# Rescheduling the first batch of a fused cosformer attention and gated MLP over four engines

## Chip, cores and metric

One core of a Trainium2 chip runs the whole program. The metric is device time in microseconds (us), the median of several runs. The engines named below are TensorE (PE, with its weight loads as PEld), VectorE (DVE), ScalarE (ACT), GpSimd (POOL) and SyncE (SP), which issues most of the DMAs.

## The reference

Linear attention with a cosine weighting, for 8 batches of 8 heads, 576 positions and 64 dimensions, all in fp32, is followed by a two-layer MLP on 4608 tokens of 512 features, with 2048 hidden units:

```
theta = pi/2 * pos/576
phi(x) = concat(relu(x)*cos(theta), relu(x)*sin(theta))        # 64 -> 128
kv  = phi(k)^T @ v        z = sum over positions of phi(k)
x   = (phi(q) @ kv) / (phi(q) . z + 1e-6)                        # per head, heads joined to 512
h   = x @ w_in;  g = h * sigmoid(beta*h);  out = g @ w_out
```

## The kernel before

**Layout.** Positions of a batch are written p*9 + n, with p in 0..63 and n in 0..8. A "block" is one n: 64 positions of each of two head groups g on 128 partitions. Heads come as two head pairs jp (0 and 1) with two heads jj each, times the two groups g. Tokens go through the MLP in 9 chunks of 512, that is 8 blocks; block 8 of batch 0 therefore already belongs to chunk 1.

**Attention of a batch.** `q_relu` and `k_relu` write bf16 relus of q and k (`qb`, `rk`). `v_scale` multiplies v by the cosine or the sine and writes `vb`; the 65th column of `vb` holds the weight itself and so gives z. `kv_mm` multiplies `rk` by `vb` on PE, with 64x64 tiles, into PSUM banks 6 and 7, and `kv_take` copies that to `kv`. `q_turn_pe` transposes `qb` on PE; its `take` functions copy the result to `qt` (ACT) and, multiplied by the tangent `tanr`, to `qs` (DVE). `num_mm` makes numerator and denominator of one block and head pair. `x_rden` adds epsilon to the denominator and inverts it, and `x_mul` (DVE) or `x_mul_act` (ACT) multiplies. `x_turn_pe` transposes the result on PE, and a copy by ACT or DVE brings it to `xt`, the MLP's input.

**MLP.** `h_mm` makes one of 16 h groups of a chunk (four 512-column matmuls, L374), in PSUM bank `h_bank`; `h_act` applies SiLU on ACT (L381). `o_part` makes the output: part i uses w_out i (16 matmuls at L399 over four token tiles). The weights are loaded as fp32 in four pieces each of w_in and w_out (1 MB each) into four stage buffers, cast to bf16 by `cast_win` (L106, L108) and `cast_wout` (L115, L117, which also divide by beta). `cast_win` has four calls for a piece, one for each combination gj of row halves.

**Order.** `manual_schedule` keeps each engine's instructions in program order, so the order written out by hand from L429 to L539 is the schedule; the framework adds the waits. Batch 0 is done first, up to chunk 0's first h groups. The first half of h groups 0 to 3 (head pair 0, `mis` 0 and 1) runs ahead of the second. Then a loop of 32 slots makes chunk 0: slots 0 to 15 are h groups, slots 16 to 31 output tiles. The dictionary `early` puts batch 1's work behind given slots. From chunk 1 on, `att_units` does the same for the later batches, and x reaches `xt` by DMA transposes. That part is untouched.

**Fill-ins.** `warm_pe(count, w)` issues matmuls on zeros that nobody reads, to keep PE busy (L424). SP issues all loads in order. Before w_in 1 and before w_in 2 stands a load of two elements into `gate` (L462, L464) that reads `rk`; SP waits for that relu and so delays the weight loads behind it. A w_out piece reuses a stage buffer and waits for the casts of the w_in piece in it.

Of the kernel before, what the change touches and what calls it, by code (L numbers as in the profile page):

```python
# [22 lines left out]
def kernel(  # L23
# [114 lines left out]
    for g in range(2):  # L138
        nc.gpsimd.iota(it9[g * HP : (g + 1) * HP], pattern=[[1, NQ]], base=0, channel_multiplier=NQ,
                       allow_small_or_imprecise_dtypes=True)  # L140
    halfpi = const.tile([P, 1], FP32, name="halfpi")
# [13 lines left out]
    zeros = const.tile([P, 512], BF16, name="zeros")  # L155
    nc.vector.memset(zeros, 0.0)
    ones = const.tile([HP, P], FP32, name="ones")
    nc.vector.memset(ones, 1.0)
# [4 lines left out]

    gate = const.tile([1, 2], BF16, name="gate")
# [12 lines left out]

    tdiag = const.tile([HP, NQ, HP], FP32, name="tdiag")
    nc.vector.tensor_tensor(  # L179
        tdiag, identf.unsqueeze(1).to_broadcast([HP, NQ, HP]),  # L180
        tan9[0:HP].unsqueeze(2).to_broadcast([HP, NQ, HP]), op=ALU.mult)
# [240 lines left out]
    def warm_pe(count, w=512, bank=1):  # L422
        for i in range(count):
            nc.tensor.matmul(ps[:, bank, 0:w], lhsT=zeros[:, 0:P], rhs=zeros[:, 0:w], start=True, stop=True)  # L424
# [37 lines left out]
    nc.sync.dma_start(out=gate, in_=rk[0:1, 0, 0, 0:2])  # L462
# [26 lines left out]
    got2 = x_rden(6, 0, 7, NQ, (1,))  # L489
# [13 lines left out]
    for i in range(1, 4):  # L503
        for f in (0, 256) if i == 1 else (0,):
            for gj in GJ:
                cast_win(i, gj, "dve", f, f + 256 if i == 1 else 512)
    load_w("out", 0)
    load_w("out", 1)
    load_raw(1, "v")
    load_raw(1, "k")  # L510
    load_w("out", 2)
    load_raw(1, "q")
    load_w("out", 3)
    cast_wout(0)
    cast_wout(1)
    v_scale(1, 0)
    k_relu(1)
    cast_wout(2)
    q_relu(1, 0)


    def num_seven(jp, bank):
        for n in range(7):
            num_mm(n, jp, bank, n)

    takes = []
    early = {
        4: lambda: x_turn_pe(0, 8, 9, 7),
        15: lambda: v_scale(1, 1, eng="act"),
        22: lambda: (kv_mm(1, 0, 6), kv_mm(1, 1, 6), q_relu(1, 1), kv_take((0, 1), 6)),  # L530
        24: lambda: (cast_wout(3, "aadd"), takes.append(q_turn_pe(1, 0, 4, hold=True))),
        25: lambda: (takes.append(q_turn_pe(1, 1, 6, hold=True)),
                     [takes[jp](e, i) for jp in range(2)
                      for e, i in (("act", 0), ("dve", 1), ("act", 1), ("dve", 0))]),
        28: lambda: (num_seven(0, 4), num_seven(1, 6), x_mul(x_rden(4, 0, 0, 7, (0,)), 0, 7)),
        29: lambda: (x_turn_pe(1, 0, 7, 4, ("act",), (0,)), x_mul(x_rden(6, 0, 0, 7, (1,)), 0, 7)),
# [91 lines left out]
```

## Time and profile before

| what | us |
|---|---|
| median of 7 runs | 299.25 (298.02 to 301.81) |
| profiled execution, its time | 298.59 |
| profiled execution, its span | 296.8 |
| PE busy in the span | 284.6 |
| first kv matmul (L268) starts | 12.99 |
| first h matmul (L374) starts | 18.48 |
| casts of w_in on DVE (L108) | 20.24 to 30.67 |
| first output matmul (L399) starts | 34.91 |
| w_out 3 lands | 45.13 |

The profile shows one execution. Times are counted from the span's start. In the page, busy shares are given for the whole span and for 40 slices of 7.4 us each; the chain of waits follows the last instruction back to what released it, step by step, as start and duration in us. A timeline row gives start, duration, engine, line, operation, output<-inputs, shape and count, and in brackets the idle time before it with what ended it. A row of the waits gives who waited for whom: us in total, times, longest. [...] many records overlap: 512-column matmuls of 379 ns start 216 ns apart.

### The profile page before, as it was taken

The numbers are of one execution on the slowest core, as the hardware profiler recorded it, in microseconds if no ns is written. First come the engines' busy times: TensorE is split into PE (matmuls) and PEld (weight loads), VectorE is DVE, ScalarE is ACT, GpSimd is POOL, SyncE is SP. The second block draws the span as 40 slices with busy tenths as digits, with TensorE's granted clock in tenths as the row PEclk, the third lists the DMA queues.
The fourth block names the chain that finished last, engine by engine and source line by source line (L and its number), as shares of the span: only waits on it lengthen the run. The fifth ranks groups of instructions, "written<-read, shape, count | busy, mean of one in ns | idle before, by whom it ended". The sixth has DMA issues, their size and how long they took to land.

```text
span 296.8 us, 7162 instructions
## 1 busy us (share of the span) xinstructions
PE 284.6 (96%) x3042; PEld 143.2 (48%) x3068; DVE 113.8 (38%) x282; ACT 140.9 (47%) x224; POOL 73.7 (25%) x88
## 2 busy tenths in 40 slices
PE   7969999999999999999999999999999999999994
PEld 5644455445444544445445544554455444444443
DVE  3879968572930195008600770068005000000000
ACT  6658836572148313841285127602761177127511
POOL 1550001443364034501460157014701210000000
PEclk9999999999999999999999999999999999999998
DMA  7999999698899059934993499229201910131033
GB/s 244 380 376 343 390 389 390 223 245 313 137 254 389 6 97 201 358 128 94 190 360 142 91 210 371 111 60 189 53 2 31 161 35 0 38 78 28 0 73 71
DMA packets 50264, 53.82 MB, mean 181 GB/s; under 512 B 30888, under 2 KB 31160, under 8 KB 50232
## 3 DMA queue, kind: packets, MB, share of 16 engines
q1 hardware_dynamic: 47512, 46.01, 51.7%
q0 software_dynamic: 2688, 7.34, 10.3%
q8 instruction: 24, 0.39, 0.5%
q14 instruction: 8, 0.07, 0.1%
q10 hardware_dynamic: 32, 0.01, 0.0%
HBM read 36.71 MB, written 9.44 MB: 155 GB/s over the span
## 4 chain that ended last, share of the span: by engine, by line
PE 93%; ACT 3%; issue 2%; DVE 1%; DVEq 0%; ACTq 0%
PE ps L374 41%; PE ps L399 39%; PE ps L289 4%; PE ps L268 3%; PE ps L424 1%; PE ps L415 1%; ACT g_t L381 1%; PE ps L238 1%; PE ps L348 1%; PE ps L432 1%; DVE qs L226 1%; ACT xt L353 1%; ACT L151 0%; DVE tdiag L179 0%; ACT wout L115 0%
## 5 line engine op out<-in xcount | busy, mean ns | idle before, releaser
L374 PE MATMUL ps<-xt,win 128*128 128x512 bf16 x576 | 127.8, 379 | 2.5 <-ACT xt L353 1.1
L399 PE MATMUL ps<-wout,g_t 128*128 128x512 bf16 x536 | 120.4, 379 | 2.3 <-issue 1.5
L381 ACT ACTIVATE g_t<-ps,beta 128x512 bf16<-128x512 f32 x144 | 98.4, 688 | 36.2 <-PE ps L374 36.2
L374 PEld LDWEIGHTS <-win 128*128 128x128 bf16 x576 | 55.6, 98 | 68.7 <-issue 1.8
L399 PEld LDWEIGHTS <-g_t 128*128 128x128 bf16 x560 | 54.0, 98 | 64.2 <-issue 0.5
L394 POOL DMA_DIRECT2D out_dram<-o_sb x56 | 35.0, 629 | 146.3 <-ACT o_sb L405 146.3
L405 ACT COPY o_sb<-ps 128x512 f32<-128x512 f32 x35 | 20.5, 586 | 99.0 <-PE ps L399 99.0
L226 POOL TENSOR_TENSOR qs<-qt,tanr 128x1152 bf16<-128x1152 bf16 x12 | 29.2, 2454 | 9.5 <-DVE vb L223 8.4
L280 DVE CAST kv<-ps 128x520 bf16<-128x520 f32 x7 | 4.9, 699 | 68.4 <-PE ps L268 68.4
L418 DVE COPY o_sb<-ps 128x256 f32<-128x256 f32 x1 | 0.4, 425 | 63.2 <-PE ps L415 63.2
L311 DVE TENSOR_TENSOR xs<-ps,rden 128x768 bf16<-128x768 f32 (+3 forms) x24 | 22.4, 935 | 1.0 <-DVE rden L304 0.2
L223 DVE TENSOR_SCALAR vb<-raw_v,cos 128x256 bf16<-128x256 f32 x63 | 17.1, 346 | 0.0
L300 DVE TENSOR_TENSOR den<-ps,eps 128x12 f32<-128x12 f32 (+3 forms) x25 | 4.1, 164 | 32.4 <-PE ps L289 32.2
L223 DVE TENSOR_SCALAR vb<-raw_v,sin 128x256 bf16<-128x256 f32 x54 | 14.7, 348 | 0.0
L289 PEld LDWEIGHTS <-qt 64*64 64x64 bf16 x576 | 10.5, 106 | 4.4 <-issue 3.9
L289 PE MATMUL ps<-kv,qt 64*64 64x65 bf16 x576 | 11.7, 195 | 0.3 <-DVE qs L226 0.2
L289 PE MATMUL ps<-kv,qs 64*64 64x65 bf16 x576 | 11.6, 193 | 0.2 <-issue 0.2
L198 DVE TENSOR_SCALAR qb<-raw_q 128x1152 bf16<-128x1152 f32 x15 | 10.6, 748 | 1.4 <-DMA raw_q<-in_q_dram 1.4
L289 PEld LDWEIGHTS <-qs 64*64 64x64 bf16 x576 | 10.5, 105 | 0.3 <-issue 0.3
L108 DVE CAST win<-w_stage 64x512 bf16<-64x512 f32 (+2 forms) x20 | 10.0, 501 | 0.4
L268 PEld LDWEIGHTS <-rk 64*64 64x64 bf16 x576 | 8.5, 106 | 3.4 <-issue 2.5
L198 DVE TENSOR_SCALAR rk<-raw_k 128x2304 bf16<-128x2304 f32 (+1 forms) x8 | 9.9, 1242 | 0.4 <-DMA raw_k<-in_k_dram 0.4
(58 smaller groups left out, 102.5 us busy)
## 6 DMA issues: line engine op xcount, KB each, us to landing
raw_v<-in_v_dram SPq DMA_DIRECT2D x7, 1152.0 KB, 9.9
raw_k<-in_k_dram SPq DMA_DIRECT2D x7, 1152.0 KB, 14.3
raw_q<-in_q_dram SPq DMA_DIRECT2D x7, 1152.0 KB, 7.3
out_dram<-o_sb POOLq DMA_DIRECT2D x56, 128.0 KB, 3.9
w_stage<-in_moe_w_out_dram SPq DMA_DIRECT2D x4, 1024.0 KB, 8.8
w_stage<-in_moe_w_in_dram SPq DMA_DIRECT2D x3, 1024.0 KB, 6.3
out_dram<-o_sb SPq DMA_DIRECT2D x14, 128.0 KB, 2.3
raw_q<-in_q_dram SPq DMA_DIRECT2D x2, 576.0 KB, 3.9
```

The source lines that it names most:

```text
L108: nc.vector.tensor_copy(o, a)
L198: nc.vector.tensor_scalar(dst, src, scalar1=0.0, scalar2=None, op0=ALU.max)
L223: nc.vector.tensor_scalar(o, a, scalar1=t[:, n : n + 1], scalar2=None, op0=ALU.mult)
L226: eng.tensor_tensor(dst.rearrange("q n (g p) -> q n g p", g=2), src.rearrange("q n (g p) -> q n g p", g=2), tanr[:, n0:n1].unsqueeze(2).to ...
L268: nc.tensor.matmul(t[jj * HP : (jj + 1) * HP, g], lhsT=rk[hs, n, 2 * jp + jj, :], rhs=vb[hs, n, 2 * jp + jj].rearrange("q s e -> q (s e)") ...
L289: nc.tensor.matmul(ps[cols, bank + jj, slot * E : (slot + 1) * E], lhsT=(qt, qs)[cs][rows, jp, n, cols], rhs=kv[rows, g, jp, cs, :], start ...
L311: nc.vector.tensor_tensor(o.rearrange("q j n s d -> q j (n s) d"), nv[:, :, a:z, :, 0:D].rearrange("q j n s d -> q j (n s) d"), rden[:, :, ...
L374: nc.tensor.matmul(ps[:, h_bank(c, jt)], lhsT=win[jt // 4][:, mi, (jt % 4) * P : (jt % 4 + 1) * P], rhs=xt[:, :, jp, g * HP : (g + 1) * HP ...
L381: nc.scalar.activation(g_t, ps[:, h_bank(c, jt)], AF.Silu, scale=beta[:, jt : jt + 1])
L394: eng.dma_start(out=out_v[bb, n][:, m0:m1], in_=o_sb[hf * HP : (hf + 1) * HP, m0:m1])
L399: nc.tensor.matmul(o_ps, lhsT=gs[c, jt][:, tt * P : (tt + 1) * P], rhs=wout[jt // 4][:, jt % 4, :], start=(jt == 0), stop=(jt == JT - 1))
L405: nc.scalar.copy(o_sb, o_ps)
```

## The change

The whole change lies in batch 0's part, in the setup ahead of it, and in the slots of chunk 0.

- Setup: `zeros` is filled in two pieces, the first ahead of the other constants. `ones` and `tdiag` go: the tangent is spread over partitions by nine fp32 PE transposes of a broadcast column, and DVE, not ACT, copies it to `tanr`. Both first q relus are on DVE.
- Dummies: 58 of 48 columns instead of 78 of 40; 8 instead of 5 of 128 columns ahead of the first turn; 7 instead of 9 of 512 columns ahead of the first kv; two more before the second x turn.
- k relu of heads 0 and 1 is split between ACT and DVE. POOL's second product with the sine covers blocks 0 to 4; ACT does blocks 5 to 8. kv of head pair 1 is made one head at a time.
- Block 8 leaves the first part: only block 7 is made beside blocks 0 to 6. Block 8's `num_mm` comes after slot 3 and its turn after slot 7 in bank 6. Its sum and product stand on DVE ahead of the casts of w_in 2 and 3. w_in 2 is cast in halves.
- The `gate` loads go; w_in 1 to 3 are issued right behind w_in 0.
- Batch 1: `kv_take` is on ACT; w_out 3 is cast one part on ACT and three on DVE, between the takes of head pair 0 and those of head pair 1, and no longer ahead of both; the second `num` comes after slot 29, the x turn of pair 0 after slot 30.

```diff
+    zeros = const.tile([P, 512], BF16, name="zeros")
+    nc.vector.memset(zeros[:, 0:P], 0.0)
...
-    zeros = const.tile([P, 512], BF16, name="zeros")
-    nc.vector.memset(zeros, 0.0)
-    ones = const.tile([HP, P], FP32, name="ones")
-    nc.vector.memset(ones, 1.0)
+    nc.vector.memset(zeros[:, P:512], 0.0)
...
-    tdiag = const.tile([HP, NQ, HP], FP32, name="tdiag")
-    nc.vector.tensor_tensor(
-        tdiag, identf.unsqueeze(1).to_broadcast([HP, NQ, HP]),
-        tan9[0:HP].unsqueeze(2).to_broadcast([HP, NQ, HP]), op=ALU.mult)
...
-    warm_pe(78, 40)
-    q_relu(0, 0, "act")
+    warm_pe(58, 48)
     for bank, n0, n1 in ((6, 0, 5), (7, 5, NQ)):
-        nc.tensor.matmul(ps[:, bank, 0 : (n1 - n0) * HP], lhsT=ones,
-                         rhs=tdiag[:, n0:n1, :], start=True, stop=True)
+        for n in range(n0, n1):
+            nc.tensor.matmul(ps[:, bank, (n - n0) * HP : (n - n0 + 1) * HP],
+                             lhsT=tan9[0:HP, n : n + 1].to_broadcast([HP, P]), rhs=identf,
+                             is_transpose=True, start=(n == n0), stop=(n == n1 - 1))
+    nc.tensor.transpose(ps[:, 1, 0:JT], beta16, identf[0:JT, 0:JT])
     for bank, n0, n1 in ((6, 0, 5), (7, 5, NQ)):
-        nc.scalar.copy(tanr[:, n0:n1, :].rearrange("q n p -> q (n p)"), ps[:, bank, 0 : (n1 - n0) * HP])
-    nc.tensor.transpose(ps[:, 1, 0:JT], beta16, identf[0:JT, 0:JT])
+        nc.vector.tensor_copy(tanr[:, n0:n1, :].rearrange("q n p -> q (n p)"), ps[:, bank, 0 : (n1 - n0) * HP])
+    q_relu(0, 0)
+    nc.vector.tensor_copy(beta, ps[:, 1, 0:JT])
     nc.vector.tensor_copy(ps[:, 0, 0:NQ], cos9)
     nc.vector.tensor_copy(ps[:, 0, 16 : 16 + NQ], sin9)
-    nc.vector.tensor_copy(beta, ps[:, 1, 0:JT])
+    q_relu(0, 1)
+    warm_pe(8, 128, bank=0 + 2)
+    q_turn_pe(0, 0, 4)
     nc.vector.reciprocal(rbeta, beta)
-    q_relu(0, 1, "dve")
-    warm_pe(5, 128)
-    q_turn_pe(0, 0, 4)
     warm_pe(4, 128)
     take = q_turn_pe(0, 1, 2, hold=True)
-    warm_pe(9)
+    warm_pe(7)
     take("act", 0)
+    take("dve", 1)
     v_scale(0, 1, 0, eng="pool")
+    take("act", 1)
     v_scale(0, 0, 0)
-    k_relu(0, 0, 2, "act")
-    take("dve", 1)
+    k_relu(0, 0, 2, "act", 0, 5)
+    k_relu(0, 0, 2, "dve", 5, NQ)
     take("dve", 0)
-    take("act", 1)
     kv_mm(0, 0, 6)
-    v_scale(0, 1, 1, eng="pool")
+    v_scale(0, 1, 1, 0, 5, eng="pool")
     v_scale(0, 0, 1)
     kv_take((0,), 6, eng="act")
+    v_scale(0, 1, 1, 5, NQ, eng="act")
     k_relu(0, 2, 3, "act")
-    k_relu(0, 3, 4, "dve", 0, 5)
-    k_relu(0, 3, 4, "act", 5, NQ)
-
-    nc.sync.dma_start(out=gate, in_=rk[0:1, 0, 0, 0:2])
-    load_w("in", 1)
-    nc.sync.dma_start(out=gate, in_=rk[0:1, 0, 3, 0:2])
-    load_w("in", 2)
-    load_w("in", 3)
-    warm_pe(1, bank=1)
-    for n in range(7, NQ):
-        num_mm(n, 0, 4, n - 7)
+    for i in range(1, 4):
+        load_w("in", i)
+    warm_pe(1)
     for n in range(7):
         num_mm(n, 0, 2, n)
-    kv_mm(0, 1, 6)
+    num_mm(7, 0, 4, 0)
     warm_pe(2, bank=1)
-    got2 = x_rden(4, 0, 7, NQ, (0,))
+    kv_mm(0, 1, 6, (0,))
+    k_relu(0, 3, 4, "act", 5, NQ)
     got = x_rden(2, 0, 0, 7, (0,))
+    got2 = x_rden(4, 0, 7, 8, (0,))
+    k_relu(0, 3, 4, "dve", 0, 5)
+    kv_mm(0, 1, 6, (1,))
+    x_mul_act(got2, 7)
     kv_take((1,), 6, eng="act")
     x_mul(got, 0, 7)
-    x_mul_act(got2, 7)
-    x_mul_act(got2, 8)
-    for n in range(7, NQ):
-        num_mm(n, 1, 6, n - 7)
     for n in range(7):
         num_mm(n, 1, 0, n)
+    num_mm(7, 1, 6, 0)
     for gj in GJ:
-        cast_win(0, gj, "pool", jps=slice(0, 1))
+        cast_win(0, gj, "act" if gj == (1, 1) else "pool", jps=slice(0, 1))
...
     x_turn_pe(0, 0, 8, 2, jps=(0,))
-    got2 = x_rden(6, 0, 7, NQ, (1,))
     got = x_rden(0, 0, 0, 7, (1,))
     x_mul(got, 0, 4)
     x_mul(got, 4, 7)
-    x_mul_act(got2, 7)
+    x_mul(x_rden(6, 0, 7, 8, (1,)), 7, 8)
+    warm_pe(2, bank=3)
+    x_turn_pe(0, 0, 4, 4, ("act",), (1,))
     h_mm(0, 0, (0, 1))
-    x_turn_pe(0, 0, 4, 4, ("dve",), (1,))
-    h_mm(0, 1, (0, 1))
     x_turn_pe(0, 4, 8, 5, ("act",), (1,))
-    x_mul_act(got2, 8)
-    h_mm(0, 2, (0, 1))
-    h_mm(0, 3, (0, 1))
+    for jt in range(1, 4):
+        h_mm(0, jt, (0, 1))
...
+    cast_halves(1)
+    def rest():
+        x_mul(x_rden(2, 0, 8, NQ, (0, 1)), 8, NQ)
+        cast_halves(2)
+        for gj in GJ:
+            cast_win(3, gj)
+        load_w("out", 0)
...
     early = {
-        4: lambda: x_turn_pe(0, 8, 9, 7),
+        3: lambda: (num_mm(8, 0, 2, 0), num_mm(8, 1, 2, 1), rest()),
+        7: lambda: x_turn_pe(0, 8, 9, 6),
         15: lambda: v_scale(1, 1, eng="act"),
-        22: lambda: (kv_mm(1, 0, 6), kv_mm(1, 1, 6), q_relu(1, 1), kv_take((0, 1), 6)),
-        24: lambda: (cast_wout(3, "aadd"), takes.append(q_turn_pe(1, 0, 4, hold=True))),
-        25: lambda: (takes.append(q_turn_pe(1, 1, 6, hold=True)),
-                     [takes[jp](e, i) for jp in range(2)
-                      for e, i in (("act", 0), ("dve", 1), ("act", 1), ("dve", 0))]),
-        28: lambda: (num_seven(0, 4), num_seven(1, 6), x_mul(x_rden(4, 0, 0, 7, (0,)), 0, 7)),
-        29: lambda: (x_turn_pe(1, 0, 7, 4, ("act",), (0,)), x_mul(x_rden(6, 0, 0, 7, (1,)), 0, 7)),
+        22: lambda: (kv_mm(1, 0, 6), kv_mm(1, 1, 6), kv_take((0, 1), 6, "act"), q_relu(1, 1)),
+        25: lambda: takes.append(q_turn_pe(1, 0, 4, hold=True)),
+        26: lambda: (takes.append(q_turn_pe(1, 1, 6, hold=True)),
+                     [takes[0](*t) for t in turns], cast_wout(3, "addd"),
+                     [takes[1](*t) for t in turns]),
+        28: lambda: (num_seven(0, 4), x_mul(x_rden(4, 0, 0, 7, (0,)), 0, 7)),
+        29: lambda: (num_seven(1, 6), x_mul(x_rden(6, 0, 0, 7, (1,)), 0, 7)),
+        30: lambda: x_turn_pe(1, 0, 7, 4, ("act",), (0,)),
```

More of the change, by code (lines that the diff above doesn't have):

```diff
@@ L162 @@
     make_identity(nc, ident)
-    gate = const.tile([1, 2], BF16, name="gate")
     vb = one.tile([P, NQ, 4, 2, E], BF16, name="vb")
@@ L492, with cast_halves @@
     x_mul(got, 4, 7)
-    x_mul_act(got2, 7)
+    x_mul(x_rden(6, 0, 7, 8, (1,)), 7, 8)
+    warm_pe(2, bank=3)
+    x_turn_pe(0, 0, 4, 4, ("act",), (1,))
     h_mm(0, 0, (0, 1))
-    x_turn_pe(0, 0, 4, 4, ("dve",), (1,))
-    h_mm(0, 1, (0, 1))
     x_turn_pe(0, 4, 8, 5, ("act",), (1,))
-    x_mul_act(got2, 8)
-    h_mm(0, 2, (0, 1))
-    h_mm(0, 3, (0, 1))
+    for jt in range(1, 4):
+        h_mm(0, jt, (0, 1))
     for gj in GJ:
         cast_win(0, gj, "dve", 256, 512, slice(1, 2))
-    for i in range(1, 4):
-        for f in (0, 256) if i == 1 else (0,):
+    def cast_halves(i):
+        for f in (0, 256):
             for gj in GJ:
[L506 to L519, printed above, removed]
+                cast_win(i, gj, "dve", f, f + 256)
+    cast_halves(1)
[5 more added lines that the diff above has]
+        load_w("out", 0)
+        load_w("out", 1)
+        load_raw(1, "v")
+        load_raw(1, "k")
+        load_w("out", 2)
+        load_raw(1, "q")
+        load_w("out", 3)
+        cast_wout(0)
+        cast_wout(1)
+        v_scale(1, 0)
+        k_relu(1)
+        cast_wout(2)
+        q_relu(1, 0)
     def num_seven(jp, bank):
@@ L526 @@
     takes = []
+    turns = (("act", 0), ("dve", 1), ("act", 1), ("dve", 0))
     early = {
-        4: lambda: x_turn_pe(0, 8, 9, 7),
+        3: lambda: (num_mm(8, 0, 2, 0), num_mm(8, 1, 2, 1), rest()),
+        7: lambda: x_turn_pe(0, 8, 9, 6),
         15: lambda: v_scale(1, 1, eng="act"),
-        22: lambda: (kv_mm(1, 0, 6), kv_mm(1, 1, 6), q_relu(1, 1), kv_take((0, 1), 6)),
-        24: lambda: (cast_wout(3, "aadd"), takes.append(q_turn_pe(1, 0, 4, hold=True))),
-        25: lambda: (takes.append(q_turn_pe(1, 1, 6, hold=True)),
-                     [takes[jp](e, i) for jp in range(2)
-                      for e, i in (("act", 0), ("dve", 1), ("act", 1), ("dve", 0))]),
-        28: lambda: (num_seven(0, 4), num_seven(1, 6), x_mul(x_rden(4, 0, 0, 7, (0,)), 0, 7)),
-        29: lambda: (x_turn_pe(1, 0, 7, 4, ("act",), (0,)), x_mul(x_rden(6, 0, 0, 7, (1,)), 0, 7)),
+        22: lambda: (kv_mm(1, 0, 6), kv_mm(1, 1, 6), kv_take((0, 1), 6, "act"), q_relu(1, 1)),
[6 more added lines that the diff above has]
+        30: lambda: x_turn_pe(1, 0, 7, 4, ("act",), (0,)),
         31: lambda: ([h_mm(1, jt, (0, 1)) for jt in range(2)], x_turn_pe(1, 0, 7, 5, ("dve",), (1,)),
```

## The prediction

> **What bounds the kernel now.** I read four views in this order: the page's busy shares and slices, the chain of waits, the timeline of 12 to 50 us, and TensorE's and SP's lists of waits.
>
> ```profile
> PE 284.6 (96%) x3042; PEld 143.2 (48%) x3068; DVE 113.8 (38%) x282; ACT 140.9 (47%) x224; POOL 73.7 (25%) x88
> PE   7969999999999999999999999999999999999994
> DMA  7999999698899059934993499229201910131033
> PE 93%; ACT 3%; issue 2%; DVE 1%; DVEq 0%; ACTq 0%
> ```
>
> TensorE (PE) is full from the fifth slice (30 us) on, so only the first 60 us can change. Full is not useful: up to 17 us PE fills with dummies (L424). The end moves by as much as the dense stream of h groups moves. In the chain it is held like this:
>
> ```profile
> 10.33 2.73 PE ps L424 x8
> 13.06 0.66 PE ps L268 x36
> ...
> 17.41 1.02 ACT xt L353
> ...
> 21.07 0.23 ACT xs L321
> ...
> 24.55 0.71 ACT g_t L381
> ```
>
> ```profile
> PE ps L374 <- ACT xt L353: 1.1, 1, 1.1
> PE ps L374 <- ACT xs L321: 0.9, 1, 0.9
> PE ps L348 <- ACT g_t L381: 0.4, 1, 0.4
> ```
>
> First, the dummies end at 13.06, though the inputs of the first kv product (L268) are ready at 11.8 (the longest, ScalarE's relu, runs 10.63 to 11.80). Second, h waits for the first x copy (18.43). Third, h group 2 writes bank 6, which ScalarE's multiply for block 8 (L321) still reads until 21.29. Fourth, the turn of block 8 uses bank 7 and waits for h group 3's activation.
>
> ```profile
> 20.24 10.43 DVE L108 CAST win<-w_stage 64x256 bf16<-64x256 f32 x20
> 30.70 3.26 DVE L117 TENSOR_SCALAR wout<-w_stage,rbeta 128x512 bf16<-128x512 f32 x8
> ```
>
> ```profile
> SPq L462 <- ACT rk L196: 5.0, 1, 5.0
> ```
>
> VectorE (DVE) casts w_in from 20.24 to 30.67 without a break. h group 12, the first to need w_in 3, starts at 31.45: cover of only 0.8 us. This second front decides what an earlier PE is worth. SP, last, sits 5.0 us in front of its first gate load before it may issue w_in 1.
>
> [...] 512-wide dummies start 427 ns apart until 12.03 us, then 216. [...] Here landings come in order of issue, even with deep backlog (w_out 0 27.54, w_out 1 30.37, v 33.64, k 36.65, w_out 2 39.34, q 42.41, w_out 3 45.13). [...]
>
> **The change, part by part** (times of the profiled execution: span 296.8, 298.59 with what lies around it, 0.66 below the median 299.25).
>
> *Opening.* VectorE loses the 0.75 us product `tdiag` and the `ones` fill. Nine fp32 transposes replace two fp32 products (4.31 to 6.59); they can start at 3.46, after `tan9`. No row shows their price. Below: 0.107 each, the spacing of a 128-wide weight load at half clock. Above: 0.33 (fp32 load of L432) + 0.285 (L436's matmul), not overlapped, 0.6 each. I take 0.16, since loads overlap matmuls in every row here: nine end at 4.9. VectorE then copies `tanr` (0.49 + 0.43, from L418's 425 ns for 256) and does the first q relu (0.70, was 1.16 on ScalarE) by 6.2. The first turn starts at 6.27 against 7.56, the second at 7.66 against 8.95. Dummies: 7 from 8.85, at half clock 7 x 0.427, end at 11.84. ScalarE's and VectorE's shares of k relu (about 0.74 and 0.42) end by 11.3, POOL's product at 11.2. So the first kv runs at **11.85 against 12.99**: 1.15 earlier. The smaller dummy and constant moves are free: they stand before the first transpose or under the wait for it.
>
> *kv of pair 1.* ScalarE takes kv at 12.7 to 13.1, then four new v scalings: [...] 0.29 apart, to 14.25. POOL's shorter product, ended 13.1 instead of 14.04, was not what kv waited for. Behind them ScalarE has relu of head 2 (0.69, to 14.85) and part of head 3 (0.41, to 15.2). kv by single heads starts at 14.9 and ends at about 15.6, as before (15.57). **The 1.15 is spent on ScalarE here**; single heads hide only 0.3 of it. num, the turn and the x copy stand as before (copy about 17.4 to 18.4).
>
> *After num.* VectorE no longer waits for PE's turn to copy xt (idle 18.53 to 19.83, copy to 20.32). ScalarE does both copies (0.59 each), by 20.2. VectorE adds block 7's sum, inverse and product (0.15 + 0.18 + 0.29) and begins casting at **19.1 against 20.24**. Without block 8 in bank 6, the first halves of h 0 to 3 end their issue at 20.75 against 22.19. Block 8's num (16 small matmuls, 0.14) is new between h groups and waits 0.2 for bank 2, in place of the 0.52 wait in bank 7. h group 5 starts at 23.7 against 25.41: 1.7 earlier.
>
> *Casts.* VectorE now has block 8's sum and product in the middle (0.17 + 0.19 + 0.42 and gaps, 0.8), and w_in 2 in eight halves (8 x 0.44) instead of four (4 x 0.71): 0.7 more. w_in 3 ends at 19.1 + 10.43 + 1.5 = 31.0 against 30.67. PE would be at group 12 at 29.75. It waits: its second matmul, which needs the last cast, runs at 31.0 against 31.67. **Of 1.7 us, 0.7 is left; w_in 3 is what is late next.**
>
> *w_out, batch 1.* q lands at 42.4 and w_out 3 at 45.13 as before. Before, ScalarE waits 5.8 for w_out 3 ahead of the qt copies, and num of pair 1 then stands 0.37 for `qs` (start 49.30). Now pair 0's four takes go first, 44.6 to 46.2; the casts (one on ScalarE, three on VectorE) 46.0 to 47.4; pair 1's takes to 48.75. Group o 3 needs the last cast at 47.4 and reaches it then. num of pair 1 stands 49.0. The chain wins another 0.4, as the 0.37 goes and the turns fall between o groups; a wait of about 0.3 for the x copy, behind two output copies on ScalarE, is included. The kv take on ScalarE (0.59) fills idle time.
>
> *SP's loads.* The two 2-byte gate loads and their waits go; behind them stood only w_in 1 to 3 and what follows. Those now issue from 6.8. As the queue is busy to 24.35 and in order, they land as before (18.9, 21.7, 24.35): nothing won or lost. The later loads of w_out wait for the casts: w_out 3's stage slot is freed at 31.0 for 30.67, with v, k and q queued ahead, so it is hidden.
>
> *Sum.* 0.7 + 0.4 = 1.1 us at the same clock step. [...] My steps for the kernel before, summed the same way, come out 0.4 late by group 15, so those of after probably do too: 0.4 more. **1.5 us: 297.1 for a profiled execution like this one, 297.7 as a median.**
>
> **Rivals.** A change of 0.5% (1.5 us) is about what a measurement can tell from none.
>
> *Forecast, 0.45:* gain 1.1 to 2.2, both sides of that bound.
>
> *The casts take nearly all, 0.25.* If VectorE starts casting at 19.7 rather than 19.1, group 12 runs at 31.6 against 31.67; the tail's 0.4 is left: 298.9. For it: ten VectorE instructions stand on the way to 19.1, and L198 took 477 ns for 320 elements beside POOL, which could lengthen k relu. Against: VectorE's 1.3 us idle is real and goes.
>
> *PE's gain stays, 0.13.* If casts run faster or w_in 3 is reached in time, the whole 1.7 and the 0.4 remain: 297.2. Against: 10.43 us of casts without a gap.
>
> *Slower, 0.17: the opening transposes.* At 0.6 each unoverlapped they end at 8.9. The q relu queued behind `tanr` on VectorE then ends at 9.8, the dummies run into 14.9, casts start at 22.1, group 12 at 34.0: 1.9 behind, 301.1. The loss is then one for one; it starts where one transpose takes over 0.38, beyond which VectorE starts casting after 20. [...] Against: L436's weight load took 178 ns, not 330.
>
> *The loads are not in order after all* (inside the 0.17): the early w_in loads take half the rate from v, k and w_in 0. Landing 3 us later gives +1 us. Against: the ordered landings above.
>
> **How the numbers follow.** Low end 296.4: the whole 2.1, 0.4 for an early clock step, and 0.3 for the scatter of a median. High end 300.4: it takes in the late casts, the late loads, and the slower case up to some 0.5 us for a transpose (0.9 us of loss for each 0.1 beyond 0.38). Faster by over 0.5% is a bit over half of the forecast, the case where PE's gain stays, and the better end of the casts: 0.45. Within: 0.38. Slower: 0.17.
>
> **What would show it.** The first L268 near 11.9, and pair 1's kv ending near 15.6. L108 starting near 19.1. No wait of PE on L321. A new wait PE L374 <- DVE win at 29.7 to 31.0. Nine L238-like fp32 transposes 0.11 to 0.25 apart. ACT wout waiting for no DMA. Wrong if w_in 0 lands later than 16.4, if h group 12 starts after 31.5, or if PE idles after 50 us.

## The result, and the profile after

The changed kernel takes **297.5 us** in the median (296.87 to 299.15, 25 runs), against 299.05 for the kernel before beside it (297.88 to 301.81, 62 runs): ratio **0.9949, 95% interval 0.9931 to 0.9967**, a gain of 1.5 us. A second set of runs of the unchanged new kernel (e4, below) gave 0.9927 (0.9898 to 0.9957). Two runs more than 1.5% above the fastest of their kernel, one of e11 and one of the kernel before, are left out where runs are counted by their clock.

The profiled execution of the new kernel took 298.60, which is 1.1 above its own median and level with the profiled 298.59 of before. That coincidence is the first thing to explain. The page first:

```profile
PE 283.8 (96%) x3028; PEld 143.1 (48%) x3056; DVE 115.9 (39%) x292; ACT 140.1 (47%) x221; POOL 73.8 (25%) x87
...
PE   8689899999999999999999999999999999999994
...
DMA  7999999698799069915992599139201910131033
...
PE 87%; DVE 5%; DMA 3%; issue 2%; ACT 1%; SPq 1%; DVEq 0%
```

PE is full from the sixth slice on (37 us; before, from the fifth). In the chain's shares a DMA (3%) has appeared, which was not there before, and ScalarE has fallen from 3% to 1%. The chain in order of time names them:

```profile
3.42 9.77 DMA raw_v<-in_v_dram
13.25 1.24 issue
...
15.18 1.13 PE ps L260 x34
...
30.89 0.70 DVE win L108
31.64 3.41 PE ps L366 x15
...
52.19 0.92 ACT xt L345
53.16 1.02 PE ps L366 x4
```

The head of the chain is now the load of v's second half, which landed at 13.20. (It was issued at 3.42; the chain puts the whole time since then on it.) Then comes the product of pair 1's kv (L260), and later the last cast of w_in 3 (L108), for which h group 12 (L366) waits, as forecast. What v's landing holds up is read in the timeline, where the bracket gives each engine's idle time and what ended it:

```profile
13.22 1.35 DVE L205 TENSOR_TENSOR vb<-raw_v,ps 128x1152 bf16<-128x1152 f32 x1 [1.12 <-DMA raw_v<-in_v_dram]
13.26 1.26 POOL L205 TENSOR_TENSOR vb<-raw_v,sin 128x640 bf16<-128x640 f32 x1 [2.18 <-DMA raw_v<-in_v_dram]
13.28 1.28 ACT L213 ACTIVATE vb<-raw_v,sin 128x128 bf16<-128x128 f32 x4 [1.01 <-DMA raw_v<-in_v_dram]
14.46 0.97 ACT L188 ACTIVATE rk<-raw_k 128x576 bf16<-128x576 f32 x2
...
15.18 1.11 PE L260 MATMUL ps<-vb,rk 64*64 64x130 bf16 x36 [1.62 <-DVE rden L296]
```

Three engines stood idle for 1.0 to 2.2 us waiting for that one load. The bracket of the PE row names `rden`, but the work behind it is ScalarE's: four v scalings, then the relu of k's head 2, which ended at 15.13. In nine of the profiles below the product starts 0.05 us after that relu, while `rden` ended 0.01 to 0.13 before it. PE's list of waits over the first 60 us:

```profile
PE ps L260 <- DVE rden L296: 1.6, 1, 1.6
...
PE ps L366 <- DVE win L108: 0.9, 1, 0.9
...
PE ps L366 <- ACT g_t L373: 0.5, 1, 0.5
...
PE ps L366 <- ACT xt L345: 0.2, 1, 0.2
```

The waits of before for ScalarE's `xs` (0.9), of the block turn for the activation (0.4) and of the first h group for the x copy (1.1) are gone; the 0.2 listed for an x copy is batch 1's, at 53.16. The waits for v and for the last cast have replaced them.

**Two executions must be compared at the same landing of v.** In the profiles of the changed kernel with its opening kept, pair 1's kv starts 1.98 to 2.07 us after that landing (e3: 2.27), and the landing scatters between 11.58 and 13.20. The unchanged kernel's two profiles took 298.60 with the landing at 13.20 and 297.98 at 12.47: 285.40 and 285.51 behind it. The landing was at 11.86 in the profile of before, where the first kv (12.99) held the chain and not v:

```profile
11.93 2.11 POOL L213 TENSOR_TENSOR vb<-raw_v,sin 128x1152 bf16<-128x1152 f32 x1 [0.71 <-DMA raw_v<-in_v_dram]
...
12.99 0.42 PE L268 MATMUL ps<-vb,rk 64*64 64x130 bf16 x16
```

At 11.86 the changed kernel would take about 297.3, **1.3 under the 298.59 of before**. This line through two executions is an estimate, but the spread agrees: its runs at full clock lie between 296.87 and 298.60, 1.7 us, and the landings of all the profiles with this opening span 1.6. (0.1 to 0.2 of the 1.3 arises behind h(1, 4), h group 4 of chunk 1, where the two kernels are the same: from its start to the end the profiles of all kernels take 239.9 to 240.9 us.)

### The profile page after: what moved, and what is told of

It is laid out like the page before. It is cut to its first block, busy times and chain, and to the rows that moved or that the text cites. A ratio compares the mean times of both kernels' runs of the same rounds, so it can differ in the third digit from the quotient of the medians.

```text
span 296.8 us, 7134 instructions
## 1 busy us (share of the span) xinstructions
PE 283.8 (96%) x3028; PEld 143.1 (48%) x3056; DVE 115.9 (39%) x292; ACT 140.1 (47%) x221; POOL 73.8 (25%) x87
## 4 chain that ended last, share of the span: by engine, by line
PE 87%; DVE 5%; DMA 3%; issue 2%; ACT 1%; SPq 1%; DVEq 0%
PE ps L391 40%; PE ps L366 38%; DVE win L108 4%; PE ps L281 3%; DMA raw_v<-in_v_dram 3%; PE ps L260 3%; PE ps L407 1%; SPq L78 1%; DVE xs L303 0%; ACT g_t L373 0%; DVE rden L296 0%; PE ps L230 0%; ACT xt L345 0%; DVE den L292 0%; DVE o_sb L410 0%
## 5 line engine op out<-in xcount | busy, mean ns | idle before, releaser
L366 PE MATMUL ps<-xt,win 128*128 128x512 bf16 x576 | 128.0, 379 | 1.7 <-DVE win L108 0.9
L366 PEld LDWEIGHTS <-win 128*128 128x128 bf16 x576 | 55.5, 98 | 68.2 <-DVE win L108 1.8
L386 POOL DMA_DIRECT2D out_dram<-o_sb x56 | 36.4, 654 | 143.4 <-ACT o_sb L397 142.9
L272 DVE CAST kv<-ps 128x520 bf16<-128x520 f32 x6 | 4.2, 700 | 68.1 <-PE ps L260 68.1
L303 DVE TENSOR_TENSOR xs<-ps,rden 128x768 bf16<-128x768 f32 (+5 forms) x26 | 23.1, 890 | 0.8
L292 DVE TENSOR_TENSOR den<-ps,eps 128x12 f32<-128x12 f32 (+4 forms) x26 | 4.2, 160 | 33.2 <-PE ps L281 33.1
L260 PE MATMUL ps<-vb,rk 64*64 64x130 bf16 x576 | 10.3, 218 | 2.3 <-DVE rden L296 1.6
L190 DVE TENSOR_SCALAR qb<-raw_q 128x1152 bf16<-128x1152 f32 x16 | 11.4, 752 | 1.3 <-DMA raw_q<-in_q_dram 1.3
L260 PEld LDWEIGHTS <-rk 64*64 64x64 bf16 x576 | 8.9, 106 | 6.2 <-ACT rk L188 3.2
L190 DVE TENSOR_SCALAR rk<-raw_k 128x2304 bf16<-128x2304 f32 (+2 forms) x9 | 10.9, 1211 | 0.5 <-DMA raw_k<-in_k_dram 0.5
L108 DVE CAST win<-w_stage 64x512 bf16<-64x512 f32 (+2 forms) x24 | 10.7, 447 | 0.5
```

What stands on the lines that cost most here:

```text
L108: nc.vector.tensor_copy(o, a)
L190: nc.vector.tensor_scalar(dst, src, scalar1=0.0, scalar2=None, op0=ALU.max)
L260: nc.tensor.matmul(t[jj * HP : (jj + 1) * HP, g], lhsT=rk[hs, n, 2 * jp + jj, :], rhs=vb[hs, n, 2 * jp + jj].rearrange("q s e -> q (s e)") ...
L303: nc.vector.tensor_tensor(o.rearrange("q j n s d -> q j (n s) d"), nv[:, :, a:z, :, 0:D].rearrange("q j n s d -> q j (n s) d"), rden[:, :, ...
L366: nc.tensor.matmul(ps[:, h_bank(c, jt)], lhsT=win[jt // 4][:, mi, (jt % 4) * P : (jt % 4 + 1) * P], rhs=xt[:, :, jp, g * HP : (g + 1) * HP ...
L386: eng.dma_start(out=out_v[bb, n][:, m0:m1], in_=o_sb[hf * HP : (hf + 1) * HP, m0:m1])
```

## The experiments

All times are medians. The kernel before stood at 299.41 beside the first four, 299.31 beside the next four and 298.76 beside the last.

### e1, e2: do the gate loads matter?

e1 puts them back into the changed kernel (the second reads head 2's relu, where the kernel before reads head 3's); e2 takes them out of the kernel before.

```diff
+    nc.sync.dma_start(out=gate, in_=rk[0:1, 0, 0, 0:2])
     load_w("in", 1)
+    nc.sync.dma_start(out=gate, in_=rk[0:1, 0, 2, 0:2])
     load_w("in", 2)
     load_w("in", 3)
```

> The changed kernel with the two gate loads put back, so that w_in 1 waits for head 0's relu and w_in 2 and 3 for head 2's. Theory A (w_in loads issued at 6.6 us keep the DMA engines that are ahead busy and so slow those that still carry v and k): the second half of v lands at 11.9 instead of 13.2 us, VectorE starts to cast before 18.8, and the median is 0.5 to 1.0 us under the changed kernel's 297.5. Theory B ([...] v's landing only scatters from execution to execution): no change beyond 0.3 us, and v lands anywhere between 11.8 and 13.2.

> The kernel before without the two gate loads, nothing else. Theory A: v's second half lands at about 13.2, POOL's product with it ends at 15.3 instead of 14.0, kv of pair 1 moves from 15.57 to about 15.9, and the median rises by 0.2 to 1.0 us over 299.05. Theory B, and my prediction's step on SP's loads: within 0.3 us of it.

e1: 297.77, ratio 0.9936 (0.9913 to 0.9958). e2: 301.16, ratio **1.0033** (1.0009 to 1.0057). v's second half landed at 12.73 with the gates (e1), at 12.47 and 13.20 without them (the changed kernel), at 11.33 in e2 without and at 11.86 in the kernel before with them. So the gates don't set that landing. In the changed kernel they are worth nothing measurable. In the kernel before, taking them out cost 0.3%, and 1.75 us between the medians. Neither theory had that. It comes with the clock: 19 of e2's 22 runs have a mean clock under 0.9965, against 15 of 39 beside them, and its other three runs, with a median of 298.37, are no slower than the others of before (298.86). Its profile shows what precedes the lower clock. This is PE's timeline:

```profile
18.61 0.27 PE L348 MATMUL ps<-ident,xs 128*128 128x128 bf16 x2
20.33 0.39 PE L348 MATMUL ps<-ident,xs 128*128 128x128 bf16 x2 [1.45 <-issue]
```

PE stops for 1.45 us between two transposes of one loop, and the profile shows no semaphore that the instruction after the stop waits for. A stop of 0.32 stands at the same matmuls in the profile of before. What is special is the place: counting PE's instructions in the trace (matmuls, weight loads and five of its sequencer), 703 lie ahead of the stop in both. The section on hardware below takes this up.

### e3, e4: are VectorE's casts the bound?

e3 gives two of the four casts of w_in 3 to GpSimd. e4 is the changed kernel once more.

```diff
-            cast_win(3, gj)
+            cast_win(3, gj, "pool" if gj[0] else "dve")
```

> The changed kernel with two of the four casts of w_in 3 on POOL, which has nothing to do from 20 to 50 us. Theory C (VectorE's casts decide when h group 12 runs): the wait of 0.9 to 1.1 us before it goes, VectorE is done with w_in 3 1.4 us earlier, POOL's two take about 1.2 us each from the landing at 25.4, and the median falls by 0.7 to 1.0 us to about 296.7. Rival D (the time is held by the landings of batch 1, so that an earlier h group only waits later): within 0.3 us of 297.5.

> The changed kernel once more, as a control and for a second profile: median 297.2 to 297.9. If v's second half lands at about 12 us in this profile, VectorE starts casting near 18.4 and the execution takes about 297.3; if at about 13.2, near 19.6 and 298.6. Under theory A it is at 13 us each time.

e3: 297.65, ratio 0.9927 (0.99 to 0.9955). e4: 297.29, ratio 0.9927 (0.9898 to 0.9957); with v at 12.47 its casts start at 18.89, between the two cases that were forecast for it. In e3's profile VectorE's casts end 11.94 after their start, in e4's 11.99, though two of 0.69 were taken away. This is the reason, VectorE's groups from 24.99 to 27.39, with GpSimd casting from 24.73 to 27.10, and in the 1.3 us after it:

```profile
L108 DVE CAST win<-w_stage 64x512 bf16<-64x512 f32 x3 | 2.7, 914 | 0.1
...
L108 DVE CAST win<-w_stage 64x512 bf16<-64x512 f32 x3 | 1.3, 423 | 0.1
```

The same cast takes 423 ns alone, 914 in the mean of three of which two ran beside GpSimd's (1.17 and 1.15 us). So the work moved to GpSimd came back as time on VectorE. As the stream of casts did not get shorter, e3 decides nothing between theory C and rival D; e13, below, does shorten it.

### e10, e11, e12: dummies and the clock

e10 adds four dummies ahead of pair 1's kv and two ahead of its numerators. e11 takes all dummies of the gaps out. e12 puts dummies into the gaps of the kernel before.

```diff
 e10, the changed kernel
-    warm_pe(2, bank=1)
+    warm_pe(6, bank=1)
     kv_mm(0, 1, 6, (0,))
...
     x_mul(got, 0, 7)
+    warm_pe(2, bank=1)
 e11, the changed kernel
-    warm_pe(1)
...
-    warm_pe(2, bank=1)
...
-    warm_pe(2, bank=3)
 e12, the kernel before
+    warm_pe(4, bank=1)
     kv_mm(0, 1, 6)
...
+    warm_pe(4, bank=3)
     h_mm(0, 0, (0, 1))
+    warm_pe(2, bank=2)
     x_turn_pe(0, 0, 4, 4, ("dve",), (1,))
+    warm_pe(3, bank=2)
     h_mm(0, 1, (0, 1))
```

> The changed kernel with six instead of two 512-column dummies ahead of the kv products of pair 1 (0.86 us more at full clock, into a wait of 0.5 to 1.6 us in the three profiles) and two more ahead of the numerators of pair 1 (0.43 us into a wait of 0.47). Clock theory: the clock falls back to half for a window of 3.41 us when TensorE idles for about 1.9 us or more of the window before (1.9 in the profile that fell back, 1.8 in the one that did not), and that is what makes the upper group of times (298.85 to 299.15, mean clock 0.993 to 0.994, 5 of 26 runs). Then no run is left with a mean clock under 0.9965, the median falls by about 0.2 to 297.2 and the highest time is below 298.6. Rival (the waits' length sets the time, the clock does not matter): dummies that fill a wait change nothing where v is late and delay the kv products by up to 0.4 where it is early, so 297.5 to 297.9, with a spread as before.

> The changed kernel without the five 512-column dummies in the gaps between 12 and 19 us (one ahead of the first numerators, two ahead of kv pair 1, two ahead of the first h). Clock theory: the window around 13 to 17 us then holds 0.6 us more idle time, 2.4 or more of 3.41, so nearly every run falls back for a window, mean clock 0.994 or 0.989, and the median rises by 1.3 to 2.5, to 298.8 to 300.0. Rival (the dummies fill waits only and the clock does not matter): 297.3 to 297.7.

> The kernel before with dummies put into its gaps: four ahead of the kv products of pair 1, four ahead of the first h, two and three around the block transposes after it, where its profile shows waits of 1.1, 0.32 and 0.89 us. Clock theory: its runs with a mean clock of 0.989 to 0.994 (15 of 39 beside the last call, median 299.7 to 300.9 against 298.86 for the others) go, so the median falls from 299.4 to about 298.8, a ratio of 0.998, and the highest time to about 299.6. If the whole gain of the change came through the clock, it would be 297.5. Rival: the dummies delay the kv products and h, 299.5 to 300.5.

e10: 298.35 (0.9965, 0.9948 to 0.9982). e11: 298.61 (0.9973, 0.9951 to 0.9995). e12: 301.33 (1.0055, 1.0029 to 1.008). Runs with a mean clock under 0.9965: 1 of 22 in e10, 6 of 21 in e11, 6 of 35 in the unchanged kernel (both sets). The order is that of the clock theory, more dummies and fewer fallbacks, but so few runs tell only e10 from e11, and e11 was forecast to fall back in nearly every run. The clock is not the time's main term either: e10 is 0.9 slower than the changed kernel although its clock hardly falls, and e11's runs at full clock have a median of 298.33, also 0.9 above. So both theories failed for both runs. e10's rival has the direction, dummies that PE must issue first stand ahead of kv when v is early, but its range ended at 297.9, and no profile shows it: in e10's, with v at 13.11, kv starts 1.99 after the landing as in the unchanged kernel. Why e10's runs and e11's runs at full clock are slower is open; e11's profiled execution (297.10 with v at 12.08) shows nothing.

In e12 the rival is right in direction and too small (299.5 to 300.5). The kernel before had no wait ahead of pair 1's kv, so four dummies there delayed it: kv 16.22 against 14.85 (0.35 of it is there at the first kv already), first h 20.85 against 18.48, casts 22.55 against 20.24. Between kv and h PE also stood for 1.23 with no semaphore shown; the profile of before has 0.32 of that, behind the first h. The runs at 0.992 and under, 9 of 39 and 11 of 58 beside the first two sets, went to 0 of 14 (4 stay at 0.993 to 0.994), but that was worth less than the delay.

### e7: the order of batch 1's start

```diff
 the changed kernel with before's slots 22 to 31, among them
-        25: lambda: takes.append(q_turn_pe(1, 0, 4, hold=True)),
+        24: lambda: (cast_wout(3, "aadd"), takes.append(q_turn_pe(1, 0, 4, hold=True))),
```

> The changed kernel with the kernel before's steps of slots 22 to 31 (the start of batch 1: ScalarE sharing the cast of w_out 3, the kv copy on VectorE, both numerators in slot 28, the x turn in slot 29). Prediction's step: the new order was worth 0.4, so this is 0.4 slower, about 297.9. Rival, from the time between h 12's second product and h(1, 4), 26.28 in both profiles with the old order and 26.5 in three with the new: the new order costs 0.23, so this is 0.2 faster, 297.2, and that stretch takes 26.3.

e7: 297.73, ratio 0.9937 (0.9914 to 0.9959), not told apart from the changed kernel by time. The rival fell: from h group 12's second product to h(1, 4) e7 takes 27.30 us, not 26.3, and the changed kernel 26.51. PE's list of waits for e7 has the wait that the prediction had said would go:

```profile
PE ps L281 <- DVE qs L218: 0.7, 1, 0.7
```

In the kernel before it was 0.2 (L289). The old order didn't get worse. The head came forward, q and w_out 3 still landed at 42.4 and 45.1, and so PE stood longer at that wait. The new order is what keeps the earlier head from being given back here. In time that is 0.8 us of one profile and 0.2 to 0.4 between the medians.

### e8, e9, e14: what lies between v and kv

e8 gives GpSimd the whole second sine product again. e9 spreads the tangents by the two fp32 products with ones, as before, for which VectorE first builds `tdiag`. e14 shortens ScalarE's part behind the landing.

```diff
 e8
-    v_scale(0, 1, 1, 0, 5, eng="pool")
+    v_scale(0, 1, 1, eng="pool")
-    v_scale(0, 1, 1, 5, NQ, eng="act")
 e9
-        for n in range(n0, n1):
-            nc.tensor.matmul(ps[:, bank, (n - n0) * HP : (n - n0 + 1) * HP],
-                             lhsT=tan9[0:HP, n : n + 1].to_broadcast([HP, P]), rhs=identf,
-                             is_transpose=True, start=(n == n0), stop=(n == n1 - 1))
+        nc.tensor.matmul(ps[:, bank, 0 : (n1 - n0) * HP], lhsT=ones,
+                         rhs=tdiag[:, n0:n1, :], start=True, stop=True)
 e14
-    v_scale(0, 1, 1, 0, 5, eng="pool")
+    v_scale(0, 1, 1, 0, 6, eng="pool")
...
-    v_scale(0, 1, 1, 5, NQ, eng="act")
-    k_relu(0, 2, 3, "act")
+    v_scale(0, 1, 1, 6, NQ, eng="act")
+    k_relu(0, 2, 3, "act", 0, 5)
+    k_relu(0, 2, 3, "dve", 5, NQ)
+    k_relu(0, 3, 4, "dve", 0, 5)
...
-    k_relu(0, 3, 4, "dve", 0, 5)
```

> The changed kernel with the second sine product of v for pair 1 whole on GpSimd again (2.11 us in one piece, as in the kernel before) and none of it on ScalarE; the kv products stay split by heads. Theory (v's landing sets it): the first kv product of pair 1 starts 2.9 us after the landing, not 1.98, which is 0.9 later, so the median rises to 298.3. Rival (the prediction's step: this part only keeps ScalarE's chain from being the last, GpSimd's product ends beside it, worth nothing): 297.4 to 297.6.

> The changed kernel with the tangents spread by the two fp32 matrix products with ones over the diagonal table, as in the kernel before, in place of the nine transposes (VectorE builds the table first). Prediction's step: the transposes bring the first kv product 1.15 earlier together with VectorE's copies; undone alone, it starts 0.5 to 1.0 later, near 11.6 to 12.0. If that counts to the end: 298.0 to 298.5. Rival (v's second half lands at 11.6 to 13.2 and is the last thing that pair 1 waits for): 297.4 to 297.7, with the first kv product later and pair 1 still 2.0 after the landing.

> The changed kernel with the chain behind the landing of v's second half shortened: GpSimd scales six of nine blocks of it and ScalarE three (5 and 4 before), the relu of k's head 2 is shared by ScalarE (five blocks) and VectorE (four), and VectorE does its part of head 3 ahead of the denominators. Theory (the landing of v's second half sets the time: in seven profiles of the changed opening the first kv product of pair 1 starts 1.98 to 2.27 us after it, and the executions spread by 1.6 us as that landing does): ScalarE's part falls from 1.28 + 0.67 to about 0.95 + 0.40, so that product starts 1.5 to 1.65 after the landing, everything up to block h(0,12) moves 0.3 to 0.4 earlier, and the median is 297.1. Rival 1 (k's last quarter, landing 0.7 to 1.6 us after v's half, sets it 0.5 us behind itself): no gain, 297.4 to 297.6. Rival 2 (VectorE's numerators x denominators, now behind two relus, are late for the block transposes, which wait for xs 0.2 to 0.4 us already): 297.6 to 298.0.

e8: 297.6 (0.9959, 0.9945 to 0.9974). kv starts 2.23 after the landing (12.67, 14.90), not 2.9: GpSimd's 2.1 us product ends only 0.25 behind where ScalarE's chain would have. So the rival stands, and the 2.9 was too high: splitting that product is worth 0.25 in the profile and nothing that the medians show.

e14: 297.19 (0.9953, 0.9936 to 0.997). The median is near the 297.1 of the theory, but the ratio doesn't tell e14 from the changed kernel, and only the theory's first half held: kv starts 1.59 after the landing (12.53, 14.12). The gain was gone two steps later, as its timeline shows:

```profile
14.12 1.24 PE L260 MATMUL ps<-vb,rk 64*64 64x130 bf16 x36 [0.36 <-POOL vb L205]
...
15.28 0.52 ACT L313 ACTIVATE xs<-ps,rden 128x64 bf16<-128x64 f32 x2 [0.81 <-DVE rden L296]
15.69 0.38 ACT L270 CAST kv<-ps 128x260 bf16<-128x260 f32 x1
...
16.11 0.22 PE L281 MATMUL ps<-kv,qt 64*64 64x65 bf16 x4 [0.76 <-ACT kv L270]
```

VectorE's inverses, now behind two relus, came late, as rival 2 had it. ScalarE's two `xs` products wait for them 0.81, and the copy of kv, queued behind those on ScalarE, starts 0.33 after PE was done. The numerators start 3.58 after the landing; in the changed kernel it was 3.56. VectorE's casts start 6.43 after it, against 6.41. Beside the bound that was shortened stood a second one.

e9: **302.4**, ratio 1.0126 (1.0099 to 1.0153), five us slower than the changed kernel and far outside what either theory had. Its first kv starts at 12.81, 1.7 later than in the profile after. Then, in PE's timeline:

```profile
15.90 0.70 PE L266 MATMUL ps<-vb,rk 64*64 64x130 bf16 x19 [0.50 <-ACT rk L194]
18.51 0.69 PE L266 MATMUL ps<-vb,rk 64*64 64x130 bf16 x17 [1.92 <-issue]
```

PE stops for 1.92 us in the middle of one kv product, again with no semaphore shown, and this time with 447 of its instructions ahead of the stop: 256 fewer than 703. The window of the clock in which it stopped was followed by one at half clock, and all six runs of e9 have a mean clock of 0.994 or less. By the profile, v landed at 11.59 and would have let pair 1's kv start at about 13.6; it starts at 15.90, 2.3 late, and from there to VectorE's casts it is 6.96 us where the changed kernel has 4.43: 2.5 more, 1.9 of it the stop; the rest I put down to the half clock. The two make up the 5 us.

### e13: block 8 back in the opening

```diff
-    num_mm(7, 0, 4, 0)
+    for n in range(7, NQ):
+        num_mm(n, 0, 4, n - 7)
...
+    x_mul_act(got2, 8)
...
-    x_mul(x_rden(6, 0, 7, 8, (1,)), 7, 8)
+    x_mul(x_rden(6, 0, 7, NQ, (1,)), 7, NQ)
...
-        x_mul(x_rden(2, 0, 8, NQ, (0, 1)), 8, NQ)
...
-        3: lambda: (num_mm(8, 0, 2, 0), num_mm(8, 1, 2, 1), rest()),
-        7: lambda: x_turn_pe(0, 8, 9, 6),
+        3: lambda: rest(),
+        4: lambda: x_turn_pe(0, 8, 9, 7),
```

> The changed kernel with block 8 summed and scaled in the opening again (ScalarE for pair 0, VectorE for pair 1, turned in slot 4) instead of between the h groups. Its cost in the cast stream goes: the eight half casts of w_in 2 take 2.5 us with it in between and 1.8 without, so casts start about 0.1 to 0.2 later and end 0.5 to 0.6 earlier, and h(0,12)'s second product, which waits for the last of them 1.0 us, starts 0.5 earlier: 297.1. Theory of the change (block 8 out of the opening is what lets the casts and h start earlier): casts and h start 0.5 to 1.0 later than with it, and the time is 297.8 to 298.4.

e13: **296.87** (296.58 to 297.06, 6 runs), ratio 0.9937 (0.992 to 0.9953): the lowest of all. The theory of the change falls for this part. VectorE's timeline, first of the changed kernel, then of e13:

```profile
19.61 4.84 DVE L108 CAST win<-w_stage 64x256 bf16<-64x256 f32 x12
...
25.23 6.35 DVE L108 CAST win<-w_stage 64x512 bf16<-64x512 f32 x12
```

```profile
18.98 11.14 DVE L108 CAST win<-w_stage 64x256 bf16<-64x256 f32 x24
```

With block 8 in between, the 24 casts take 11.98 from start to end; without it 11.14. They start 6.56 after v's landing in e13 and 6.41 in the changed kernel, so keeping block 8 out of the opening gained 0.15 and cost 0.84 in the stream that h group 12 waits for. e13's profiled run ends 284.3 behind the landing, against 285.4 and 285.5. Up to h(1, 4) that is 44.26 behind the landing against 44.95 and 44.97, or 0.7, which is 0.84 less 0.15; the rest arises behind it, in unchanged code. By the intervals against before e13 isn't told apart from the changed kernel (0.9949 and 0.9927); one profile is what speaks for it.

This also answers the question of e3: with 0.84 less in VectorE's stream, h group 12's second product comes 0.68 earlier behind the landing (17.76, 18.44), so the casts are what it waits for. Against the 10.43 of the kernel before, e13's casts still take 0.71 longer, the price of casting w_in 2 in halves; no run casts it whole.

## Why the prediction was right, and where its steps were not

The forecast was 297.7 (296.4 to 300.4), by a gain of 1.5; measured are 297.5 and 1.5. Step by step, at v's landing of 11.86 (each time of the profile after less 1.34):

- **The transposes: the rival fell, the size was near.** Nine took 1.19 us, 0.12 apart (0.16 taken, 0.38 the point of loss), and the first turn came at 5.92 (6.27). The first kv started at 11.13 in the profile itself. That is not the case of the 11.85, where dummies at half clock end last, but that of an early clock step: the full clock came at 9.39, the dummies ended near 10.5, and the inputs decided (11.3 forecast). The 12.99 of before, too, belongs to a late step, at 12.02; in e2, with before's opening and the step at 9.48, it is 11.86. At a like step this part brought 0.7 us, not 1.15. e9 shows 1.7 us for the transposes undone.
- **"The 1.15 is spent on ScalarE here": wrong as to what holds pair 1.** ScalarE did use the time ahead up, but not by being busy: it stood idle 1.0 us for v. (One of the four new scalings took 0.390 to 0.407.) The sum had taken the landing from one execution (11.86) as fixed, and left out that an earlier first kv makes this load the last input. With the landing at 11.86 kv would have ended at 14.95, not 15.6.
- **Casts start at 19.1: at that landing 18.27.** h group 5 then comes 2.6 earlier than before, not 1.7. Of the 2.0 that the casts gain, 1.0 is there at pair 1's kv (13.84 against 14.85). The rest lies between kv and the casts, where ScalarE makes both x copies; no run undoes that by itself.
- **"Of 1.7 us, 0.7 is left; w_in 3 is what is late next": the mechanism held.** The casts took 11.98 from their start (11.93 predicted), PE waited 0.9 for the last one, and h group 12's second product came at 30.30, a gain of 1.4 and not 0.7. This is the term that was mis-sized, by the start of the casts.
- **"The chain wins another 0.4" in batch 1: the sign failed in the sum.** From h group 12's second product to h(1, 4) the kernel before took 26.28 and the changed one 26.51: a loss of 0.23. The wait for `qs` went, as said, but the x copy on ScalarE cost PE 0.23 and the turns added short gaps. The old order would have been worse (27.30 in e7's one profile), as q's landing doesn't come forward with the head. I had set the change against the old wait of 0.37, not against what that wait becomes.
- **"0.4 more" for my own bias** stood in for none of this, and was not needed: 1.4 less 0.2, and 0.2 later in the stream, make the 1.3 that the two profiles give at one landing.
- **The gate loads "nothing won or lost": right for the weights, incomplete for the queue.** At the same landing of v, w_in 3 comes at 24.1 (25.42 in the profile; 24.35 forecast). In the kernel before the gates did matter: without them PE's stop of 0.32 became 1.45 (e2). What links the two was not shown.
- **Two signs of being wrong came up.** w_in 0 landed at 17.41 and not by 16.4, as the whole queue came later in this execution, v by 1.34. And PE idles after 50 us, 0.23 for the x copy. h group 12 started at 30.35, under 31.5.
- **The clock:** only the step's time was in the sum. That the clock falls back was not. Of the runs whose clock is on record, 32 of 112 of the kernel before have a mean clock under 0.9965, and 21 are at 0.992 or under; of the changed one 6 of 35, and 1. Among runs at full clock the medians are 298.6 to 298.9 and 297.3 to 297.4, so 1.2 to 1.6 us is there without it. The median of all runs lies 0.1 to 0.6 above that of the full-clock runs for the kernel before, and under 0.1 for the changed one: fewer fallbacks are the rest of the gain.

So the path was right, through the casts of w_in 3 to h group 12, but that the total fits to the tenth is luck: its terms were wrong in opposite directions, the casts' gain too small, batch 1's and the bias too large. The reading by single executions hid both, as the profile before and after took the same time.

## What to carry over

Before a chain is shortened, look up which load lands next behind it, and take its landing from several executions: part of the gain can end there. Work moved out of the opening into the gaps of another engine's stream is paid in that stream if something waits for its end; sum both places. In a stretch of many small matmuls, count PE's instructions too: the next section's four stops had 447, 703 or 705 of them ahead, and with a change in the opening (e9), the dummies (e12) or the queued loads (e2) PE stopped for 1.23 to 1.92 us, where the kernel before has 0.32.

## What the runs showed of the hardware

**PE stopped four times with no semaphore shown, each time behind a packet of the instruction queue.** The stops of over 0.3 us without a semaphore in the first 60 us come with 703 (kernel before, e2), 705 (e12) and 447 (e9) instructions ahead, 256 apart to within two. The trace has a DMA queue of kind "instruction", 24 packets of 16 KB in the whole program, and one of them stands ahead of the end of each stop. This is that queue's row (packets, MB, share) in the DMA view of e9 from 15.9 to 17.3 us:

```profile
q8 instruction: 1, 0.02, 4.8%
```

In e9 the packet ran from 16.07 to 17.14 and PE went on at 18.51; in e2 17.89 to 18.94 and 20.33; in e12 17.43 to 18.51 and 19.98; in the kernel before 16.91 to 17.96 and 19.50. PE goes on 1.4 to 1.5 us after the packet's end each time, and in no profile does it pass one of these places (447, 703 and on in steps of 256, in the first 50 us) sooner than that after a packet; e13, which does not stop, passes 703 1.6 us after it, and the changed kernel 2.9 (20.24 and 23.13).

Counted on from those places in steps of 256, the packet ahead of 703 begins 2.2 to 2.4 us after PE passes 447 in the three profiles with gate loads and 3.2 to 4.3 after it in the eleven without; the one ahead of e9's stop at 447 begins 5.5 after PE passes 191. From such a place to the stop at the next lie 3.7 to 6.1 us in the four profiles that stop, among small matmuls and with 1 MB loads in the queues, and the stops lasted 0.32 to 1.92 us. The changed kernel passes the places at 7.7, 15.5 and 23.1, has 7.6 to 7.8 us between them and shows no such stop. In e2, where the gates were taken out and the stop grew from 0.32 to 1.45, PE also passed 447 1.1 us earlier.

The 24 packets stand against 6,110 matmuls and weight loads of PE (kernel before), about 255 to each; that one packet goes with each 256 instructions is an estimate from this and the counts ahead of the stops. That PE waited for these packets was not shown: no run tested it, only the four stops and their packets speak for it. The counts can be off, as the trace of the kernel before has 536 output matmuls (L399) for 560 of their weight loads.

**The clock fell back while PE was in use.** Besides those at the end of the span, half-clock windows of 3.41 us came after the step to full clock in four of fourteen profiles. These are e1's and e2's windows of the clock, in steps of 3.41: the stretch, its length, PE's busy time, then the other engines, the clock, DMA and GB/s:

```profile
13.24:16.65 3.41, 1.47 (x81) 1.30 (x84) 2.75 (x7) 2.89 (x9) 1.77 (x3) 1.00 1.05 387
16.65:20.06 3.41, 3.19 (x59) 2.22 (x49) 2.78 (x10) 1.83 (x3) 2.46 (x6) 0.50 0.98 328
20.06:23.50 3.44, 3.41 (x19) 1.60 (x18) 3.26 (x9) 1.87 (x4) 0.00 (x0) 1.00 1.01 363
```

```profile
16.31:19.72 3.41, 1.48 (x36) 0.90 (x25) 1.77 (x6) 1.63 (x4) 2.65 (x6) 1.00 1.05 390
19.72:23.13 3.41, 1.91 (x9) 1.06 (x10) 2.20 (x7) 1.01 (x3) 0.00 (x0) 0.50 0.96 350
23.13:26.55 3.42, 3.42 (x9) 1.18 (x8) 3.25 (x8) 0.74 (x2) 0.00 (x0) 0.50 0.80 275
```

In all fourteen profiles, a full-clock window after the step in which PE was busy for 1.34 to 1.48 us (e1, e2, e8, e9), 39 to 43% of it, is followed by one at half clock, and none with 1.60 or more is. e2's next window, at half clock and busy for 1.91, is followed by another at half. At the end of the span the half clock follows windows with PE busy for 0.81 us (kernel before, 291.93 to 295.34) and 0.00 (changed kernel, 292.69 to 296.11). In e1, e2, e8 and e9 the time in which PE stood was followed by a half-clock window on top of it.

**VectorE's casts took longer beside GpSimd's:** 423 ns alone, 1.15 and 1.17 us beside GpSimd's (e3), each ending 0.28 us after one of these. GpSimd's own took 1.14 and 1.19 us for 1024 elements, no more for each than in its casts of w_in 0 (0.60 to 0.61 us for 512). The size is that of one run; why it is so was not shown.

**v's second half landed at 11.3 to 13.2 us** in fourteen executions though it was issued at 2.8 to 3.7 in all of them. What decides it is open.
